# A buffer each for the two last rows, and fifteen tiny loads in the SyncE queue

## The chip, the cores and the metric

One core of a Trainium2 chip runs the whole kernel. The metric is device time in microseconds (us); several runs of one kernel are compared by their medians. A profile is one execution with the hardware profiler on; its span is the time between its first and last recorded instruction.

## The reference

A decode step of attention, forward and backward, with one query per head: 32 heads, 8192 keys and values of 128 numbers each, all bf16.

```python
B, H, Sq, Skv, Dh = 1, 32, 1, 8192, 128
scale = q.shape[-1] ** -0.5
scores = jnp.einsum('bhqd,bhkd->bhqk', q, k) * scale
attn = _softmax(scores, axis=-1)
out = jnp.einsum('bhqk,bhkd->bhqd', attn, v)
...
_out, _vjp = jax.vjp(_f, q, k, v)
return (_out, *_vjp(grad_out))     # O, dq, dk, dv
```

With p the softmax row, dp = v . dO and ds = p (dp - sum(p dp)) scale, the four results are O = p v, dq = ds k, dk = ds x q and dv = p x dO (two outer products). O and dq are 32 rows of 128 numbers, 8 KB each. K and V are read once (134 MB) and dk and dv written once (134 MB).

## The kernel before

The heads are taken in 16 pairs. A pair's K is one tile `Kt` of 128 partitions by 32 KB (4 MB), its V one tile `Vt` of the same shape; partitions 0 to 63 hold the first head, 64 to 127 the second. There are three K buffers and two V buffers. The outer products are written over the same tiles: `outer(j, "dk", r)` turns an eighth of `Kt` into dk and `outer(j, "dv", r)` an eighth of `Vt` into dv on VectorE, and behind the last eighth (or after each half, or quarter, in the first and last pairs) the finished tile is stored from SyncE (L271).

The loop `for j in range(HP + 1)` (L321) is written out by hand inside `tc.manual_schedule()`, so each engine executes in the order of the text. One turn j does the scores and the softmax of pair j, the gradient of K of pair j-1 (`p_`), and the V side of pair j. Nearly all transfers are issued from SyncE, in this order in a middle turn:

- the store of dk of pair j-1 (L271), which waits for VectorE's last `outer(p_, "dk", 7)`;
- `load_v(j + 1)` (L433, issued at L90), which waits until the store of dv of pair j-1 has landed, since it takes that buffer;
- the store of dv of pair j (L271), which waits for VectorE's last `outer(j, "dv", 7)`;
- `load_k(j + 2)` (L456, issued at L84), which waits until the store of dk of pair j-1 has landed.

SyncE's queue is in order: whatever waits there holds what stands behind it. The two loads of q and grad_out are the only transfers issued elsewhere (ScalarE, into `rows`). The built program gives its transfers eight completion counters in turn, so a transfer is issued only when the one eight issues before it (on the same counter) has landed.

Columns of O and dq gather in `o_all` and `dq_all` over the turns. The function `result(src, dst)` (L300 to L307) finishes one of them: ScalarE casts it into `half`, TensorE transposes it, ScalarE copies the 32 rows into `fin_sb` (L306), SyncE stores `fin_sb` (L307). Both `half` and `fin_sb` come from the pool `small`, which has one buffer for each name. `result(o_all, out_0)` is called in the last turn, j = 16 (L373), behind the eight `outer(p_, "dk", r)` of the last pair with their four stores of 1 MB; `result(dq_all, out_1)` follows at the end (L458).

Of the kernel before, what the change touches and what calls it, by code (L numbers as in the profile page):

```python
# [11 lines left out]
BF16 = mybir.dt.bfloat16  # L12
# [16 lines left out]
def kernel(  # L29
# [11 lines left out]
    nc = tc.nc  # L41
    P = 128
    _, H, S, D = k.shape
# [13 lines left out]
    consts = ctx.enter_context(tc.tile_pool(name="consts", bufs=1))  # L57
# [3 lines left out]
    small = ctx.enter_context(tc.tile_pool(name="small", bufs=1))  # L61
# [10 lines left out]
    def rows_of(x, j, c=0, parts=1):  # L72
        L = NT // parts
        return x[0, 2 * j:2 * j + 2].rearrange("b s d -> (b s) d").rearrange("(p n) d -> p n d", p=P)[:, c * L:(c + 1) * L, :]

    def slots(X, c, parts):
        L = NT // parts
        return X[:, c * L:(c + 1) * L, :]

    def load_k(j):  # L80
        Kt[j] = kpool.tile([P, NT, D], BF16, tag="K", name="Kt")
        parts = 4 if j == 0 else 1
        for c in range(parts):
            nc.sync.dma_start(slots(Kt[j], c, parts), rows_of(k, j, c, parts))  # L84

    def load_v(j):
        Vt[j] = vpool.tile([P, NT, D], BF16, tag="V", name="Vt")
        parts = 4 if j in (0, HP - 1) else 1
        for c in range(parts):
            nc.sync.dma_start(slots(Vt[j], c, parts), rows_of(v, j, c, parts))  # L90
# [6 lines left out]
    load_k(1)  # L97
    load_v(1)
    load_k(2)

    ident = consts.tile([P, P], BF16)
    make_identity(nc, ident[:])
# [99 lines left out]
    def v_scores(j, f):  # L202
        cols = XV[j].rearrange("p m s -> p (m s)").bitcast(BF16).rearrange(
            "p (m z s e) -> p z e m s", z=2, s=P, e=2)
        if f == 0:
            st[j]["dp"] = psD.tile([P, 512], F32, tag="dp", name="dp_ps")
        out = st[j]["dp"]
        for z in range(2):
            for e2 in range(2):
                at = 6 - 4 * f - 2 * z  # L210
                for b in range(NQ):
                    nc.tensor.matmul(out[b * QD:(b + 1) * QD, :], lhsT=do_win[:, b // 2, e2, at:at + QD],  # L212
                                     rhs=cols[:, z, e2, :, b * QD:(b + 1) * QD],
                                     start=(f == 0 and z == 0 and e2 == 0), stop=(f == 1 and z == 1 and e2 == 1),
                                     skip_group_check=True)
# [20 lines left out]
    def contract(j, which, first, last):  # L236
        X, pool = (Vt[j], psO) if which == "p" else (Kt[j], psQ)
        if first == 0:
            acc[which] = pool.tile([P, 512], F32, tag="acc", name="acc_" + which)
        for g in range(first, last):  # L240
            b = g % NQ
            nc.tensor.matmul(acc[which][b * QD:(b + 1) * QD, :], lhsT=wins[which][:, g, :],  # L242
                             rhs=X[:, 4 * g:4 * g + 4, :].rearrange("p n d -> p (n d)"),
                             start=(g < NQ), stop=(g >= NG - NQ), skip_group_check=True)
# [5 lines left out]
    def gather(j, which, bank):  # L250
        S, to = acc.pop("S" + which), (o_all if which == "p" else dq_all)
        pick = lane[:].rearrange("p (w j) -> p j w", j=4)
        at = 8 if which == "p" else 16
        for i in range(4):
            nc.tensor.matmul(bank[:, at:at + 2], lhsT=S[:, i, :], rhs=pick[:, i, 0:2],  # L255
                             start=(i == 0), stop=(i == 3), skip_group_check=True)
        nc.scalar.copy(to[:, 2 * j:2 * j + 2], bank[:, at:at + 2])

    def outer(j, which, r):
        x = st[j]  # L260
        G, dst = (Kt[j], out_2) if which == "dk" else (Vt[j], out_3)
        rep, row = x["ds"] if which == "dk" else x["p"], qd[j][:, 0 if which == "dk" else 1, :]
        nc.vector.tensor_tensor(  # L263
            slots(G, r, NU).rearrange("p n (a b) -> p n a b", b=R),
            slots(rep, r, NU).unsqueeze(2).to_broadcast([P, CH, D // R, R]),
            row.rearrange("p (a b) -> p a b", b=R).unsqueeze(1).to_broadcast([P, CH, D // R, R]),
            op=ALU.mult)
        parts = PARTS.get((which, j - HP), 2 if j < SPLIT else 1)
        if r % (NU // parts) == NU // parts - 1:
            c = r // (NU // parts)  # L270
            nc.sync.dma_start(rows_of(dst, j, c, parts), slots(G, c, parts))  # L271
# [26 lines left out]
        window("ds", ds1[:].rearrange("p (g j) -> p g j", j=4))  # L298

    def result(src, dst):  # L300
        half = small.tile([P, H], BF16, tag="half", name="half")
        nc.scalar.copy(half[:], src[:])
        fin_ps = psT.tile([P, 2 * TB, P], BF16, tag="T", name="fin_ps")
        nc.tensor.transpose(fin_ps[0:H, 0, :], half[:], ident[:])
        fin_sb = small.tile([H, D], BF16, tag="fin", name="fin_sb")
        nc.scalar.copy(fin_sb[:], fin_ps[0:H, 0, :])  # L306
        nc.sync.dma_start(dst.rearrange("b h s d -> (b h s) d"), fin_sb[:])  # L307

# [3 lines left out]
    def chunk(j, c):  # L312
        v_transposes(j, c)
        v_copy(j, c)
# [6 lines left out]
    for j in range(HP + 1):  # L321
# [50 lines left out]
        if j == HP:  # L372
            result(o_all, out_0)  # L373
            gather(p_, "ds", st[p_]["m"])
            break
# [53 lines left out]
        if not ends:  # L429
            for r in range(4, NU):  # L430
                outer(p_, "dk", r)
            if j + 1 < HP:
                load_v(j + 1)  # L433
        for r in range(NU):
            if early:
                contract(j, "p", 4 * r, 4 * r + 4)
                if 3 <= r < NU - 1:
                    for c in range(NC + 2 * r - 6, NC + 2 * r - 4):
                        if c > NC + 2:
                            chunk(j, c)  # L440
                if r == NU - 1:
                    v_scores(j, 1)
                    gather(p_, "ds", x["m"])
            else:
                for c in (2 * r, 2 * r + 1):
                    if j > 0 or c > 2:
                        chunk(j, c)
                contract(j, "p", 4 * r, 4 * r + 4)
                if r % 4 == 3:
                    v_scores(j, r // 4)  # L450
            outer(j, "dv", r)
# [2 lines left out]
            do_window(j + 1)  # L454
        if 0 < j and j + 2 < HP:
            load_k(j + 2)  # L456

    result(dq_all, out_1)  # L458
    order.__exit__(None, None, None)

# [29 lines left out]
```

## Time and profile before

| | |
|---|---|
| median of 3 runs | 640.74 us (640.11 to 641.88) |
| the profiled execution's own time | 640.61 us |
| its span | 638.5 us |
| busy, share of the span | PE 78%, DVE 81%, ACT 35%, POOL 1% |
| DMA packets of SyncE's and ScalarE's queues | 268.46 MB in 12480, 0.02 MB in 96 |
| read and written in HBM | 134.23 MB each, 420 GB/s over the span |

The profile's page gives the busy time of each engine, then the same in 40 slices of the span with the mean busy share of the core's 16 DMA engines, then the DMA queues, the chain of work that ended last, the costliest groups of instructions, and the transfers by the line that issues them with the median time from issue to landing. "SPq" is SyncE as an issuer of transfers, and the DMA queue q1 holds what SyncE issues, q10 what ScalarE issues; q8 and q14 bring instructions. Times in the views of waits, of stretches and of the timeline are microseconds from the start of the span.

### The profile page before, as it was taken

The page shows a single profiled execution, that of the slowest core. Times are in us where ns is not written, and L with a number is a line of the kernel's source. Part 1 is how long each engine was busy: PE and PEld are TensorE (multiplying, and loading weights), DVE is VectorE, ACT ScalarE, POOL GpSimd, SP SyncE. Part 2 cuts the span into 40 slices and gives each one's busy share as a digit, 9 for nine tenths or more (in the row PEclk, how much of TensorE's full clock was granted, in tenths as well). Part 3 has the DMA queues.
Part 4 walks back from the last instruction along what each step waited for, and adds up shares of the span by engine and source line. Part 5 has one row for each costly group of instructions (what it writes and reads, how often), then busy time and mean ns, then how long its engine had stood idle before and what let it go on. Part 6 is the DMA issues. An engine that isn't in the chain of part 4 may idle for free.

```text
span 638.5 us, 8533 instructions
## 1 busy us (share of the span) xinstructions
PE 498.9 (78%) x3480; PEld 282.3 (44%) x3480; DVE 517.1 (81%) x654; ACT 222.3 (35%) x508; POOL 3.2 (1%) x10
## 2 busy tenths in 40 slices
PE   4887786878787987879788778887779877788770
PEld 1444443354453635435264443635436354353540
DVE  6579997979889798877979877798777987968872
ACT  2432434053342614316053340524316243250440
POOL 2000000000000000000000000000000000000000
PEclk9789989878698886778968697796877968897685
DMA  8999999999999999999999999999999999999985
GB/s 365 436 437 405 440 424 431 415 424 435 437 429 431 428 428 431 432 441 430 426 427 429 443 432 429 426 430 439 434 432 426 429 438 427 436 431 422 404 371 220
DMA packets 12614, 269.01 MB, mean 421 GB/s; under 512 B 1568, under 2 KB 1568, under 8 KB 1568
## 3 DMA queue, kind: packets, MB, share of 16 engines
q1 hardware_dynamic: 12480, 268.46, 98.2%
q8 instruction: 27, 0.44, 0.3%
q14 instruction: 11, 0.09, 0.0%
q10 hardware_dynamic: 96, 0.02, 0.0%
HBM read 134.23 MB, written 134.23 MB: 420 GB/s over the span
## 4 chain that ended last, share of the span: by engine, by line
DMA 35%; PE 34%; DVE 23%; ACT 4%; issue 3%; DVEq 0%; SPq 0%; ACTq 0%
DMA Kt<-in_k_dram 19%; DMA out_dram<-Kt 15%; PE s_ps L178 13%; PE T_ps L195 9%; DVE Kt L263 8%; DVE XK_sb L168 6%; DVE Vt L263 4%; PE acc_ds L242 4%; PE m_ps L255 3%; PE acc_p L242 3%; DMA out_dram<-fin_sb 1%; DVE sT L185 1%; PE dp_ps L212 1%; ACT XV_sb L200 1%; DVE dpT L223 1%
## 5 line engine op out<-in xcount | busy, mean ns | idle before, releaser
L263 DVE TENSOR_TENSOR Vt<-p_rep,qd 128x2048 bf16<-128x2048 bf16 x128 | 155.6, 1224 | 58.2 <-PE acc_p L242 48.9
L178 PE MATMUL s_ps<-XK_sb,q_win 128*128 128x512 bf16 x512 | 151.5, 428 | 40.1 <-DVE XK_sb L168 34.8
L195 PE MATMUL T_ps<-ident_f,Vt 128*128 128x128 f32 x1024 | 169.5, 319 | 0.0
L200 ACT COPY XV_sb<-T_ps 128x512 f32<-128x512 f32 x256 | 140.2, 591 | 81.4 <-PE T_ps L195 81.3
L168 DVE STREAM_TRANSPOSE XK_sb<-Kt 128x1024 f32<-128x1024 f32 x128 | 151.0, 1221 | 21.0 <-DMA Kt<-in_k_dram 10.8
L263 DVE TENSOR_TENSOR Kt<-ds_rep,qd 128x2048 bf16<-128x2048 bf16 x128 | 149.5, 1215 | 3.2 <-PE acc_ds L242 2.8
L195 PEld LDWEIGHTS T_ps<-ident_f,Vt 128*128 128x128 f32 x1024 | 135.5, 164 | 36.6 <-issue 22.0
L178 PEld LDWEIGHTS <-q_win 128*128 128x128 bf16 x512 | 51.2, 110 | 124.2 <-issue 92.4
L242 PE MATMUL acc_p<-Vt,win_p 128*32 128x512 bf16 x512 | 56.0, 438 | 2.9 <-ACT win_p L234 2.9
L242 PE MATMUL acc_ds<-Kt,win_ds 128*32 128x512 bf16 x512 | 44.0, 441 | 4.6 <-ACT win_ds L234 4.6
L212 PE MATMUL dp_ps<-XV_sb,do_win 128*32 128x512 bf16 x512 | 34.6, 384 | 13.5 <-ACT XV_sb L200 13.5
L248 ACT COPY S_ds<-acc_ds 128x512 f32<-128x512 f32 x16 | 9.4, 587 | 84.1 <-PE acc_ds L242 84.1
L234 ACT COPY win_ds<-ds 64x128 bf16<-64x128 bf16 x32 | 9.5, 296 | 79.0 <-DVE ds L293 78.8
L404 ACT ACTIVATE e<-sT,nbias 128x128 f32<-128x128 f32 x16 | 8.3, 516 | 69.3 <-DVE nbias L400 69.3
L255 PE MATMUL m_ps<-lane,S_ds 128*128 128x2 f32 x128 | 25.1, 318 | 4.1 <-DVE rinv L414 4.1
L212 PEld LDWEIGHTS <-do_win 128*32 128x32 bf16 x512 | 14.2, 94 | 29.2 <-issue 22.6
L405 PE MATMUL m_ps<-rs,ones_f 128*128 128x1 f32 x32 | 8.0, 318 | 24.4 <-ACT e L404 24.4
L255 PEld LDWEIGHTS m_ps<-lane,S_ds 128*128 128x128 f32 x128 | 23.7, 277 | 6.2 <-DVE rinv L414 5.2
L242 PEld LDWEIGHTS <-win_p 128*32 128x32 bf16 x512 | 13.2, 94 | 28.3 <-issue 24.8
L242 PEld LDWEIGHTS <-win_ds 128*32 128x32 bf16 x512 | 9.8, 103 | 33.1 <-issue 30.0
L391 PE MATMUL m_ps<-ident_f,top 128*128 128x128 f32 x16 | 4.8, 300 | 23.6 <-DVE top L389 23.6
L185 DVE STREAM_TRANSPOSE sT<-s_ps 128x512 f32<-128x512 f32 x16 | 11.5, 717 | 14.2 <-PE s_ps L178 14.2
(59 smaller groups left out, 206.8 us busy)
## 6 DMA issues: line engine op xcount, KB each, us to landing
Kt<-in_k_dram SPq DMA_DIRECT2D x15, 4096.0 KB, 29.3
Vt<-in_v_dram SPq DMA_DIRECT2D x14, 4096.0 KB, 29.1
out_dram<-Vt SPq DMA_DIRECT2D x11, 4096.0 KB, 29.3
out_dram<-Kt SPq DMA_DIRECT2D x10, 4096.0 KB, 23.8
out_dram<-Vt SPq DMA_DIRECT2D x10, 2048.0 KB, 22.8
out_dram<-Kt SPq DMA_DIRECT2D x10, 2048.0 KB, 20.2
Vt<-in_v_dram SPq DMA_DIRECT2D x8, 1024.0 KB, 19.7
Kt<-in_k_dram SPq DMA_DIRECT2D x4, 1024.0 KB, 7.8
```

What stands on the lines that cost most here:

```text
L168: nc.vector.transpose(XK[j, u][:].rearrange("p g w i -> p (g w i)"), slots(Kt[j], u, NU).rearrange("p g d -> p (g d)").bitcast(F32))
L178: nc.tensor.matmul(st[j]["s"][:], lhsT=q_win[:, c, at:at + P], rhs=cols[:, c // 2, c % 2], start=(u == 0 and c == 0), stop=(u == NU - 1 an ...
L185: nc.vector.transpose(sT[:].rearrange("p g r -> p (g r)"), x["s"][:])
L195: nc.tensor.transpose(T_ps[:, i, :], words[:, m * P:(m + 1) * P], ident_f[:])
L200: nc.scalar.copy(XV[j][:, b * TB:(b + 1) * TB, :], st[j].pop(("T", c))[:])
L212: nc.tensor.matmul(out[b * QD:(b + 1) * QD, :], lhsT=do_win[:, b // 2, e2, at:at + QD], rhs=cols[:, z, e2, :, b * QD:(b + 1) * QD], start= ...
L234: nc.scalar.copy(wins[which][t * M:(t + 1) * M, :, 4 * t:4 * t + 4], src[t * M:(t + 1) * M])
L242: nc.tensor.matmul(acc[which][b * QD:(b + 1) * QD, :], lhsT=wins[which][:, g, :], rhs=X[:, 4 * g:4 * g + 4, :].rearrange("p n d -> p (n d) ...
L248: nc.scalar.copy(S[:].rearrange("p j d -> p (j d)"), acc.pop(which)[:])
L255: nc.tensor.matmul(bank[:, at:at + 2], lhsT=S[:, i, :], rhs=pick[:, i, 0:2], start=(i == 0), stop=(i == 3), skip_group_check=True)
L263: nc.vector.tensor_tensor(slots(G, r, NU).rearrange("p n (a b) -> p n a b", b=R), slots(rep, r, NU).unsqueeze(2).to_broadcast([P, CH, D // ...
L404: nc.scalar.activation(e[:].rearrange("p (u g) -> p u g", u=NU), x["sn"], ACT.Exp, bias=nbias[:], scale=scale, accum_out=rs[:])
```

## The change

Two things are changed.

- `half` and `fin_sb` in `result` get two buffers each, so the rows of dq no longer use the buffers of the rows of O.
- A new function `mark()` issues from SyncE a load of two numbers (4 bytes) into each of n partitions of a new tile `marked`, with n = 1 at the first call and 15 at the fifteenth. Nothing reads `marked`. From turn 6 on it is called right behind `load_v(j + 1)` and right behind `load_k(j + 2)`, until the fifteen are used up: two in each of the turns 6 to 12 and one in turn 13.

```diff
+    marks = list(range(1, 16))
+    marked = consts.tile([16, len(marks), 2], BF16)
+
+    def mark():
+        n = marks.pop(0)
+        nc.sync.dma_start(marked[0:n, n - 1], k[0, 0].rearrange("(p n) d -> p n d", p=P)[0:n, 0, 0:2])
...
     def result(src, dst):
-        half = small.tile([P, H], BF16, tag="half", name="half")
+        half = small.tile([P, H], BF16, tag="half", name="half", bufs=2)
         nc.scalar.copy(half[:], src[:])
         fin_ps = psT.tile([P, 2 * TB, P], BF16, tag="T", name="fin_ps")
         nc.tensor.transpose(fin_ps[0:H, 0, :], half[:], ident[:])
-        fin_sb = small.tile([H, D], BF16, tag="fin", name="fin_sb")
+        fin_sb = small.tile([H, D], BF16, tag="fin", name="fin_sb", bufs=2)
...
             if j + 1 < HP:
                 load_v(j + 1)
+                if j >= 6 and marks:
+                    mark()
...
         if 0 < j and j + 2 < HP:
             load_k(j + 2)
+            if j >= 6 and marks:
+                mark()
```

The order of instructions on TensorE, VectorE, ScalarE and GpSimd is the same in both programs; SyncE has fifteen transfers more. `marked` lies ahead of the big tiles in SBUF and moves all of them up by 64 bytes.

## The prediction

> **What bounds the kernel now.** I read the page first, then the DMA share by stretches of the span, then the tail: the chain, the timeline of ScalarE, the small tile that is stored last.
>
> ```profile
> span 638.5 us, 8533 instructions
> PE 498.9 (78%) x3480; PEld 282.3 (44%) x3480; DVE 517.1 (81%) x654; ACT 222.3 (35%) x508; POOL 3.2 (1%) x10
> ...
> DMA  8999999999999999999999999999999999999985
> ...
> q1 hardware_dynamic: 12480, 268.46, 98.2%
> q8 instruction: 27, 0.44, 0.3%
> ```
>
> No compute engine is over 81% busy; the packets of SyncE's queue fill 98.2% of 16 DMA engines over the whole span. In the 40 slices only the first and the last two are under 9. So transfers bound the kernel, and a change to it can bring something only where the DMA engines stand idle, which is at the two ends. The end, by stretches (the last two columns are the DMA share and GB/s):
>
> ```profile
> core 0: us, PE busy (x) PEld busy (x) DVE busy (x) ACT busy (x) POOL busy (x), PEclk, DMA share, GB/s
> ...
> 400.00:500.00 100.00, 82.83 (x582) 48.83 (x582) 82.12 (x102) 39.43 (x87) 0.00 (x0) 0.83 1.00 429
> ...
> 621.00:629.50 8.50, 1.50 (x10) 1.16 (x10) 5.21 (x5) 1.47 (x6) 0.00 (x0) 0.63 1.01 418
> 629.50:630.60 1.10, 0.00 (x0) 0.00 (x0) 0.00 (x0) 0.00 (x0) 0.00 (x0) 0.50 0.75 304
> 630.60:633.00 2.40, 0.00 (x0) 0.00 (x0) 0.00 (x0) 0.00 (x0) 0.00 (x0) 0.50 0.16 65
> 633.00:635.30 2.30, 0.00 (x0) 0.00 (x0) 0.00 (x0) 0.00 (x0) 0.00 (x0) 0.50 0.06 25
> 635.30:636.20 0.90, 0.00 (x0) 0.00 (x0) 0.00 (x0) 0.25 (x1) 0.00 (x0) 0.50 0.00 0
> ```
>
> In the middle all 16 engines work. From 629.5 on they run dry, and from 633.0 to 635.3 the share is 0.06, one engine of 16, at 25 GB/s, which is a sixteenth of some 430. So the DMA engines do not finish together: one is still working through its part of the last stores some 4.7 us after the first ones have run out (630.6 to 635.3). I call it the late ring. Nothing but its queue sets the time up to 635.8. What stands behind it:
>
> ```profile
> 626.66 9.15 DMA out_dram<-fin_sb
> 635.81 0.02 issue
> ...
> 635.89 0.25 ACT fin_sb L306
> ...
> L307 SPq DMA_DIRECT2D out_dram<-fin_sb x2: 319/450/581, 626.7 to 636.2; - x2
> ...
> DMA to landing us min/median/max: 1.3/5.2/9.1
> ...
> SPq L485 <- DMA out_dram<-fin_sb: 1.0, 1, 1.0
> ```
>
> The rows of O (8 KB) are issued at 626.66, behind the last 1 MB store in the same rings, and land 9.15 us later, when the late ring has come to them. Only then may ScalarE copy the rows of dq into the same `fin_sb` (635.89 to 636.14); their store is issued at 636.2, lands 1.3 us later, at 637.5, and the program ends 1.0 us after that, at 638.5.
>
> **The buffers: 1.65 us off the end.** The timeline of ScalarE shows how long dq had been ready:
>
> ```profile
> 622.18 0.25 ACT L306 COPY fin_sb<-fin_ps 32x128 bf16<-32x128 bf16 x1 [0.32 <-PE fin_ps L304]
> ...
> 623.36 0.22 ACT L302 CAST half<-dq_all 128x32 bf16<-128x32 f32 x1
> 635.89 0.25 ACT L306 COPY fin_sb<-fin_ps 32x128 bf16<-32x128 bf16 x1 [12.32 <-DMA out_dram<-fin_sb]
> ```
>
> The cast is done at 623.58. The copy of O started 0.32 us after its cast, so with a buffer of its own the copy of dq is over by 624.2, before SyncE issues the rows of O at 626.66. The rows of dq are then issued right behind them, by 627.6 at the latest (626.66 and two issues, 0.58 at most each, leave that much room), and stand in the rings directly behind the rows of O. What they add there is the price of a few small packets, which the stretch after 636.2 shows, since it holds nothing but the second of these stores:
>
> ```profile
> DMA packets 48, 0.01 MB, mean 4 GB/s; under 512 B 48, under 2 KB 48, under 8 KB 48
> ...
> q1 hardware_dynamic: 48, 0.01, 1.8%
> ...
> out_dram<-fin_sb SPq DMA_DIRECT2D x1, 8.0 KB, 1.3
> ```
>
> 48 packets took 1.8% of 16 x 2.3 us, 0.66 us, or 14 ns each; three to an engine (two rows and a completion count), so 0.04 us. The rows of dq land at 635.81 + 0.04 = 635.85, the end comes at 636.85, and 638.5 - 636.85 = 1.65 us go. From both sides: if they land together with the rows of O it is 1.7, and if a landing of its own 1.3 us were still to be paid behind the first it would be 638.5 - (635.81 + 1.3 + 1.0) = 0.4. I take 1.65, since four stores in a row are seen to pass through the rings without such gaps (share 1.01 from 621.0 to 629.5). What is late next is the late ring itself; the second buffers of `half` only remove a wait that already ends at 622.
>
> **The tiny loads in the rings: 0.2 us.** Fifteen loads have 1 + 2 + ... + 15 = 120 rows of 4 bytes. The trace of before has small loads at its start, those of q and grad_out, 32 rows of 256 bytes each; in the first 6 us:
>
> ```profile
> DMA packets 294, 1.54 MB, mean 257 GB/s; under 512 B 108, under 2 KB 108, under 8 KB 108
> ...
> q10 hardware_dynamic: 92, 0.02, 1.5%
> ```
>
> 1.5% of 96 us is 1.44 us for 92 packets, 16 ns each. A ring that takes part in a tiny load has one row and one count, 2 x 14 ns = 0.03 us. In the middle of the span that time is added to rings that are never idle, so it counts; and it decides the end only for the late ring. That ring has between 0 and all 15 of them: 0 to 0.42 us, and 0.2 at the half, which I take. These are lower bounds in one respect: a 4-byte load in the middle of full rings isn't in the trace of before. The upper bound is that a ring stands still until each load has landed, 1.3 us by the row above; it is a rival below. Less than nothing is excluded: nothing is taken off any ring.
>
> The Trainium skill ("DMA: Bandwidth & Descriptors", on why a DMA increments its semaphore by 16) says that a transfer from SyncE over n rows, n up to 15, runs on n engines, the lowest-numbered. By it the lowest engine takes part in all fifteen, and the charge would be 0.42 us if that is the late ring and 0 if the late one is the highest. No view here numbers the engines, so the trace neither bears it out nor speaks against it.
>
> **The tiny loads in SyncE's queue: nothing.** Each stands behind a big load and ahead of a store, and holds the store by its issue, 0.3 to 0.6 us by the row of L307 above. A middle turn in SyncE's timeline, and what it waits for between 240 and 560 us:
>
> ```profile
> 484.09 0.33 SPq L271 DMA_DIRECT2D out_dram<-Kt  x1
> 487.18 0.34 SPq L90 DMA_DIRECT2D Vt<-in_v_dram  x1
> 497.34 0.33 SPq L271 DMA_DIRECT2D out_dram<-Vt  x1
> 506.89 0.34 SPq L84 DMA_DIRECT2D Kt<-in_k_dram  x1
> 520.51 0.33 SPq L271 DMA_DIRECT2D out_dram<-Kt  x1
> ...
> SPq L271 <- DVE Kt L263: 131.3, 9, 16.8
> SPq L84 <- DMA out_dram<-Kt: 78.9, 8, 11.5
> SPq L271 <- DVE Vt L263: 71.0, 8, 11.0
> ```
>
> Behind the V load 10 us pass to the next store, behind the K load 13.6 us, and both stores wait for VectorE (131.3 us in 9 waits, 71.0 in 8). That cover is 20 times the issue. Were it gone, 15 x 0.33 = 5 us of issue would stand in the queue, though with two or three big transfers in the rings even those would not make them idle.
>
> The second thing in that queue is the completion counters. With six transfers to a turn instead of four, "eight issues before" goes back 1.33 turns instead of 2.
>
> ```profile
> Kt<-in_k_dram SPq DMA_DIRECT2D x15, 4096.0 KB, 29.3
> Vt<-in_v_dram SPq DMA_DIRECT2D x14, 4096.0 KB, 29.1
> out_dram<-Vt SPq DMA_DIRECT2D x11, 4096.0 KB, 29.3
> ```
>
> The closest case is the store of dk, which would look back to the K load of the turn before: the turn is 36.4 us long (484.09 to 520.51), that load was issued 36.4 + 13.6 = 50 us earlier and has landed after 29.3. 20 us of room, so no wait is added, and a later issue would need a landing of 50 us to be held.
>
> The third is the place of the tiles, 64 bytes higher in SBUF. I cost it at nothing: no row prices an address. If it lengthened or shortened each of the 12480 packets by one small packet's 14 ns, it would be 12480 x 14 ns / 16 = 11 us either way.
>
> **The sum.** Against the profiled execution: 640.61 - 1.65 + 0.2 = 639.16. It lies 0.13 under the median of the runs, so the forecast is 639.3 us, 0.22% less than 640.74. About 0.3%, or 1.9 us, is what a measurement of this kernel can tell from no change, and the forecast lies inside it.
>
> **Rivals.**
>
> *Each tiny load stops its rings until it has landed.* A mechanism that ends slower. For it: the only small store that stands alone in the trace takes 1.3 us from issue to landing with 0.04 us of packets. If the late ring takes part in all fifteen and loses 1.3 each time, 15 x 1.3 = 19.5 us are added: 640.74 + 19.5 - 1.65 = 658.6. It turns the sign at 1.65 / 15 = 0.11 us for each load, and makes the kernel slower by 0.3% from (1.65 + 1.9) / 15 = 0.24 us on. Against it: the share of 1.00 in the middle, where every big transfer, too, ends in a count of a few bytes in each ring without leaving the rings idle. Chance 0.13, mostly near the turning point, 642 to 645, and not at its upper end.
>
> [...]
>
> *The second buffer frees nothing.* The rows of dq land after the rows of O by a time of their own anyway, or the late ring is another, longer one in most runs, so that the end does not shorten: 0.4 us gained, 0.2 lost, 640.5. For it: SyncE's queue is in order and the two stores share rings. Against it: the stretch of 0.9 us at share 0.00 from 635.3 on, in which the rings wait for the second store and for nothing else. Chance 0.12.
>
> *Faster by over 0.3%.* The buffers bring their upper 1.7, the late ring has none of the tiny loads, and the end is as regular as in the profile: 639.0, which is 0.27% under the median. The runs of before spread over 1.8 us (640.11 to 641.88), so a measured difference of 0.3 to 0.4% is well within reach: 638.5. Chance 0.28.
>
> **The numbers.** The forecast proper, within 0.3%, has 0.47; with the rival that frees nothing, 0.59 for "same"; faster 0.28, slower 0.13. The range starts at the lowest run less the full gain, 640.11 - 1.7 = 638.4, and ends at the rival that frees nothing, 640.5, with half the spread of the runs, 0.9, on top: 641.4. It leaves out nearly all of the rival that stops the rings.
>
> **What would show it.** After: the chain still ends in the store of `fin_sb`, but ScalarE's second copy at L306 starts before 625 with no wait for a DMA; both stores of L307 stand within 1 us, and there is no stretch of share 0.00 before the last landing; from landing to the end 1.0 us remain. The DMA share in the middle stays 1.00, and the sixteen rings run dry at the same times as before, to 0.4 us. Wrong would be: idle stretches in the rings behind the tiny loads, a wait of SyncE at the tiny loads' line, a late ring that is later by over 0.5 us, or a last landing more than 0.5 us after the rows of O.

## The result and the profile after

638.6 us (six runs, 638.49 to 639.06) against 640.58 us for the kernel before in the same comparison: ratio 0.997, 95% interval 0.9957 to 0.9983. That is 2.0 us or 0.31% less, with an interval from 1.1 to 2.8 us. The forecast was 639.3 us, 0.22% less.

The page of the changed kernel: span, the DMA share in 40 slices, the packets by size, and the queues.

```profile
span 636.6 us, 8553 instructions
...
DMA  8999999999999999999999999999999999999995
...
DMA packets 12854, 269.01 MB, mean 423 GB/s; under 512 B 1808, under 2 KB 1808, under 8 KB 1808
...
q1 hardware_dynamic: 12720, 268.46, 98.6%
q8 instruction: 27, 0.44, 0.3%
```

The span is 1.9 us shorter. SyncE's queue has 240 packets more than before (12720 to 12480), the 120 rows and 120 counts of the tiny loads, and all slices but the first and the last are at 9. The last slice but one was an 8 before; that digit is not the change's, since the page of the same kernel run again (the full change once more, below) ends in an 8 and a 6. The same stretches of the middle and the tail as in the prediction:

```profile
400.00:500.00 100.00, 82.57 (x580) 48.77 (x581) 82.12 (x102) 39.41 (x87) 0.00 (x0) 0.83 1.01 432
...
621.00:629.50 8.50, 1.90 (x9) 1.62 (x9) 2.98 (x3) 0.73 (x4) 0.00 (x0) 0.50 0.91 381
629.50:630.60 1.10, 0.00 (x0) 0.00 (x0) 0.00 (x0) 0.00 (x0) 0.00 (x0) 0.50 0.33 142
630.60:633.00 2.40, 0.00 (x0) 0.00 (x0) 0.00 (x0) 0.00 (x0) 0.00 (x0) 0.50 0.14 56
633.00:635.30 2.30, 0.00 (x0) 0.00 (x0) 0.00 (x0) 0.00 (x0) 0.00 (x0) 0.50 0.04 18
```

In the middle, with the tiny loads in the rings, the share is 1.01; at the end one ring still works alone until about 635. The timelines of ScalarE and SyncE in the changed kernel (its lines L313, L314 and L278 are L306, L307 and L271 of the kernel before):

```profile
622.84 0.22 ACT L309 CAST half<-dq_all 128x32 bf16<-128x32 f32 x1
623.43 0.25 ACT L313 COPY fin_sb<-fin_ps 32x128 bf16<-32x128 bf16 x1 [0.38 <-PE fin_ps L311]
...
617.20 7.14 SPq L278 DMA_DIRECT2D out_dram<-Kt  x4
624.44 2.12 SPq L314 DMA_DIRECT2D out_dram<-fin_sb  x2
```

The copy of dq's rows stands at 623.43 with no wait for a DMA, where it stood at 635.89; both small stores are issued one behind the other, and after them there is no further step. By the counts of completion in the trace (sixteen for each big transfer and each row store, one from each ring), the rows of O land at 635.48 and the rows of dq at 635.67, against 635.81 and 637.52 before; 0.9 us later the program ends.

### The profile page after: what moved, and what is told of

It is laid out like the page before. It is cut to its first block, busy times and chain, and to the rows that moved or that the text cites. A ratio compares the mean times of both kernels' runs of the same rounds, so it can differ in the third digit from the quotient of the medians.

```text
span 636.6 us, 8553 instructions
## 1 busy us (share of the span) xinstructions
PE 498.7 (78%) x3480; PEld 283.3 (44%) x3480; DVE 518.0 (81%) x654; ACT 221.8 (35%) x508; POOL 3.2 (0%) x10
## 3 DMA queue, kind: packets, MB, share of 16 engines
q1 hardware_dynamic: 12720, 268.46, 98.6%
## 4 chain that ended last, share of the span: by engine, by line
PE 41%; DMA 26%; DVE 23%; ACT 4%; issue 3%; DVEq 0%; ACTq 0%; SPq 0%
DMA Kt<-in_k_dram 19%; PE s_ps L185 15%; PE T_ps L202 12%; DVE Kt L270 7%; DMA out_dram<-Kt 7%; DVE XK_sb L175 7%; PE acc_p L249 4%; PE acc_ds L249 4%; PE m_ps L262 3%; DVE Vt L270 3%; PE dp_ps L219 2%; ACT XV_sb L207 2%; DVE sT L192 1%; DVE dpT L230 1%; ACT p_rep L423 1%
## 5 line engine op out<-in xcount | busy, mean ns | idle before, releaser
L202 PE MATMUL T_ps<-ident_f,Vt 128*128 128x128 f32 x1024 | 167.2, 317 | 0.8 <-DMA Vt<-in_v_dram 0.8
L202 PEld LDWEIGHTS T_ps<-ident_f,Vt 128*128 128x128 f32 x1024 | 133.7, 163 | 36.9 <-issue 20.5
L249 PE MATMUL acc_ds<-Kt,win_ds 128*32 128x512 bf16 x512 | 42.5, 427 | 4.6 <-ACT win_ds L241 4.6
L219 PE MATMUL dp_ps<-XV_sb,do_win 128*32 128x512 bf16 x512 | 34.7, 386 | 13.5 <-ACT XV_sb L207 13.5
L262 PEld LDWEIGHTS m_ps<-lane,S_p 128*128 128x128 f32 x128 | 21.4, 240 | 5.7 <-issue 2.3
```

Source lines behind the costliest of these rows:

```text
L202: nc.tensor.transpose(T_ps[:, i, :], words[:, m * P:(m + 1) * P], ident_f[:])
```

## The experiments

All ratios are to the kernel before, run on the same chip beside the experiment.

### Each half of the change by itself

The buffers alone: `bufs=2` for `half` and `fin_sb`, no `mark()`.

> The second buffers of half and fin_sb alone, no tiny loads, no tile moved. Theory A (the buffers are the whole gain, the tiny loads cost and bring nothing): ratio 0.997, as the full change, about 638.6 us; in the profile the rows of dq land 0.2 us behind the rows of O and the program ends 0.9 to 1.0 us later. Theory B (the tiny loads, or the 64 bytes by which their tile moves the others, brought some 0.3 us of it): 638.9 to 639.2 us. Theory C (the tiny loads cost what was forecast, 0.2 us on the late ring): 638.4 us. B and C lie near what five rounds can resolve; a difference of over 0.6 us from the full change would be seen.

638.93 us, ratio 0.9981 (0.9972 to 0.9990): 1.2 us less than before, between 0.6 and 1.8. The tile that is stored last, in this kernel:

```profile
L306 ACT COPY fin_sb<-fin_ps x2: 254/254/254, 623.1 to 625.7; 32x128 bf16<-32x128 bf16 x2
L307 SPq DMA_DIRECT2D out_dram<-fin_sb x2: 608/862/1115, 626.7 to 627.4; - x2
...
DMA to landing us min/median/max: 8.2/8.4/8.7
```

The first store is issued at 626.7 and lands 8.7 us later, at 635.4; the second is issued at 627.4 and lands 8.2 us later, at 635.6. So the second costs 0.2 us behind the first.

The tiny loads alone: `mark()` and its calls, `half` and `fin_sb` with one buffer.

> The fifteen tiny loads alone, one buffer each for half and fin_sb as before. Theory A: the same as before, ratio 1.000 to 0.1%, and the profile ends as before with a stretch of share 0.00, ScalarE's wait of some 12 us and a second store. Theory B (they bring 0.3 us): 640.3 us. Rival, each tiny load stops its rings until it has landed: 642 us or more.

640.35 us, ratio 1.0003 (0.9994 to 1.0012). The fifteen loads cost between -0.4 and 0.8 us, at most 0.05 us each. ScalarE's wait for the first small store is back:

```profile
635.10 0.25 ACT L313 COPY fin_sb<-fin_ps 32x128 bf16<-32x128 bf16 x1 [9.97 <-DMA out_dram<-fin_sb]
```

Then a second buffer for `fin_sb` alone, and beside it the full change once more.

```diff
-        fin_sb = small.tile([H, D], BF16, tag="fin", name="fin_sb")
+        fin_sb = small.tile([H, D], BF16, tag="fin", name="fin_sb", bufs=2)
```

> A second buffer for fin_sb alone, one for half. Theory A (only the rows that a store still reads must be kept; the cast of dq waits for the transpose of O, done at 622): the same as both buffers, 638.9, ratio 0.998. Rival (the cast of dq is late too): the second store is issued later than 0.7 us behind the first.

> The full change once more, on the chip of these runs. Theory A (the buffers are all of it): ratio 0.998 as with the buffers alone, within 0.996 to 0.9990. Theory B (the tiny loads bring 0.1% of their own): 0.997 again, below 0.9975.

`fin_sb` alone: 638.67 us, ratio 0.9977 (0.9967 to 0.9986). The full change: 638.75 us, 0.9975 (0.9966 to 0.9984). The two cannot be told apart. The gain is that of one 256-byte-wide tile's second buffer; the second `half` and the tiny loads add nothing that these runs can see. Theory B, a gain from the tiny loads, isn't borne out: the ratio did not fall below 0.9975, and the loads alone gave 1.0003.

### Three times as many tiny loads

```diff
-        nc.sync.dma_start(marked[0:n, n - 1], k[0, 0]...[0:n, 0, 0:2])
+        for i in range(3):
+            nc.sync.dma_start(marked[0:n, 3 * (n - 1) + i], k[0, 0]...[0:n, 0, 0:2])
```

> The full change with each tiny load issued three times in a row (45 loads, ten transfers to a turn). Eight issues before then goes back less than a turn: the third tiny load behind the K load looks back to the V load of the same turn, which was issued some 20 us earlier and takes some 28 us to land, so SyncE must wait there for about 8 us; the third one behind the V load looks back to the K load of the turn before and waits for some 8 us too. Theory A (the queue has cover, since the store behind waits for VectorE 8 to 14 us after the load's issue): the waits stand in the trace, at the tiny loads' line, some 100 us in total, and the time is that of the full change to 0.3%, 638 to 640.5 us. Rival 1 (the counters bind): the stores behind are issued later than VectorE is done, and the time rises by some us. Rival 2 (rings stop for each tiny load): 30 more of them cost 30 times 0.1 us or more, 641.6 us and up.

639.49 us, ratio 0.9988 (0.9979 to 0.9997); the buffers alone gave 638.93 in the same comparison, so 45 tiny loads are worth 0.6 us, 0.012 us each, which the intervals do not tell from nothing. What SyncE waited for (L107 is the tiny load, L279 the store):

```profile
SPq L279 <- DVE Kt L271: 130.4, 21, 17.7
SPq L279 <- DVE Vt L271: 107.5, 15, 12.9
...
SPq L107 <- DMA Vt<-in_v_dram: 59.3, 7, 8.6
...
SPq L107 <- DMA Kt<-in_k_dram: 58.7, 7, 8.5
```

A turn of its timeline (L84 is the K load, L90 the V load):

```profile
508.57 0.35 SPq L84 DMA_DIRECT2D Kt<-in_k_dram  x1
508.97 9.57 SPq L107 DMA_DIRECT2D marked<-in_k_dram  x3
522.89 0.37 SPq L279 DMA_DIRECT2D out_dram<-Kt  x1
528.35 0.35 SPq L90 DMA_DIRECT2D Vt<-in_v_dram  x1
528.75 9.58 SPq L107 DMA_DIRECT2D marked<-in_k_dram  x3
538.44 0.37 SPq L279 DMA_DIRECT2D out_dram<-Vt  x1
```

The completion counters do bind here: 118 us of waits at the tiny loads' line, 8.5 us at a time. They take the place of waits for VectorE at the stores, of which 238 us remain. The profiled execution, at 640.9 us the slowest of its ten, shows where SyncE waited and not what that cost. Behind the K load 4.4 us of cover were left after the wait (518.5 to 522.9), behind the V load 0.1 us. This is where the counters would begin to cost, and the change as it stands is far from it: in its own trace SyncE has no wait at that line.

### The small stores ahead of the last big one

Buffers as above, no tiny loads, and the stores of `fin_sb` issued from ScalarE; run twice.

```diff
-        nc.sync.dma_start(dst.rearrange("b h s d -> (b h s) d"), fin_sb[:])
+        nc.scalar.dma_start(dst.rearrange("b h s d -> (b h s) d"), fin_sb[:])
```

> The second buffers, no tiny loads, and the two stores of fin_sb issued from ScalarE instead of SyncE. They are then issued as soon as their copies are done, at about 621 and 624 us, ahead of the last one or two stores of dk, and in another queue. Theory A (the end is the late ring, and the two small stores stand behind the last store of dk in it): the last landing becomes that of the last store of dk, 0.37 us earlier than with the buffers alone (635.67 to 635.30 in the profile of the full change); 638.2 us against 638.6. Rival (the second queue takes turns with the first in the same rings and costs elsewhere, or the end waits for something else): no gain, 638.6 or more.

> The second buffers and the small stores issued from ScalarE once more, beside the cut store, on the same chip: 638.0, ratio 0.9966 as before, 0.995 to 0.998.

637.99 us, ratio 0.9966 (0.9954 to 0.9979), and 638.07 us, 0.9963 (0.9951 to 0.9975). Each is the lowest of its comparison among the kernels that compute everything, 0.9 us under the buffers alone. The intervals of the two versions overlap, so the difference is likely and not shown; the two profiled executions lie 0.3 us apart (638.27 and 638.56). ScalarE's timeline:

```profile
620.65 0.33 ACTq L307 DMA_DIRECT2D out_dram<-fin_sb  x1
...
622.42 0.34 ACTq L307 DMA_DIRECT2D out_dram<-fin_sb  x1
```

They land 5.2 and 4.8 us later, at about 626 and 627, and the last landing is that of the last store of dk, at 635.45, 0.1 us ahead of the last one with the buffers alone (635.57). It did not cost nothing: SyncE waited 3.1 us for the counter of a small store before its last store of dk, which the late ring hid.

### Why one ring is late

Five runs with the instructions, the transfers and the computing changed. First fewer instructions on TensorE (the contractions take only the first 4 of 32 groups):

```diff
-        for g in range(first, last):
+        for g in range(first, min(last, NQ)):
```

> The second buffers, and of the 32 matmuls of each contraction (O and dq) only the first 4; the sums over the other 28 groups of rows are left out, so O and dq are not the reference's. TensorE has 3660 instructions instead of 5452, all bytes moved by the stores and loads are the same. Theory A (one ring is late because the instructions of TensorE are fetched through it, 16 KB at a time, 21 fetches in the whole kernel that put it some 10 us behind by 600 us, 0.5 us each): the q8 line shows 20 packets instead of 27, the late ring ends some 3.5 us earlier, and the time falls by 3 to 4 us against the buffers alone (638.9), to 635 to 636. Rival 1 (the late ring is slow by itself, or late from the partitions it serves): its end stays, 638.9 to 0.5 us, although TensorE has less to do. Rival 2 (compute sets the end): the stores of the last pair are issued earlier by the matmuls saved, about 2 x 28 x 0.14 = 8 us of TensorE time for a pair, less what is hidden, and the time falls by that whatever the ring does.

637.2 us, ratio 0.9953 (0.9938 to 0.9969), 1.5 us under the full change in the same comparison, not 3 to 4. SyncE's timeline:

```profile
614.65 7.14 SPq L271 DMA_DIRECT2D out_dram<-Kt  x4
```

The queue of instruction fetches on its page:

```profile
q8 instruction: 20, 0.33, 0.2%
```

And the last stretches:

```profile
630.60:633.00 2.40, 0.00 (x0) 0.00 (x0) 0.00 (x0) 0.00 (x0) 0.00 (x0) 0.50 0.10 42
633.00:635.30 2.30, 0.00 (x0) 0.00 (x0) 0.00 (x0) 0.00 (x0) 0.00 (x0) 0.50 0.01 4
```

The last four stores are issued from 614.65 on, 4.8 us earlier than before (619.42), and the time falls by a third of that. Compute does not set the end (rival 2 falls); the late ring does. The two runs with ScalarE's stores say the same without any change of the kernel, for SyncE issued the last four stores of dk 4.3 us apart in them:

```profile
617.83 8.40 SPq L271 DMA_DIRECT2D out_dram<-Kt  x4
622.14 8.31 SPq L271 DMA_DIRECT2D out_dram<-Kt  x4
```

The last landing came at 635.45 in the first and at 635.61 in the second. By the counts in the trace of the run with fewer matmuls, the late ring's part of the last store landed at 633.9 instead of 635.2 with the buffers alone: 1.3 us earlier, with 7 fetches less. That the fetches did it, and not the stores issued earlier, this run alone does not show.

More instructions: 200 memsets of a tiny tile on GpSimd in each of 13 turns.

```diff
+        if 0 < j < 14:
+            for i in range(200):
+                nc.gpsimd.memset(idle[:], 0.0)
```

> The second buffers, and 2600 tiny memsets on GpSimd spread over the turns 1 to 13 (GpSimd is idle there and nobody waits for them). Ten more fetches of 16 KB, so the q8 line shows about 37 packets. Theory A with GpSimd's fetches in another ring than TensorE's: a ring other than the late one falls back by 5 us, the late ring stays, and the time is 638.9 to 0.3%. Theory A with both in the same ring: the late ring falls back by 5 us more, 643.5 to 644. Rival (fetches cost the rings nothing): 638.9, and the rings run dry as with the buffers alone.

642.52 us, ratio 1.0037 (1.0023 to 1.0051), 3.6 us above the buffers alone. The fetches came in another queue than expected, q14, with 31 packets instead of 11, on the page:

```profile
q14 instruction: 31, 0.25, 0.1%
```

And the last stretches:

```profile
633.00:634.30 1.30, 0.00 (x0) 0.00 (x0) 0.00 (x0) 0.00 (x0) 0.00 (x0) 0.50 0.85 332
634.30:636.00 1.70, 0.00 (x0) 0.00 (x0) 0.00 (x0) 0.00 (x0) 0.00 (x0) 0.50 0.11 44
636.00:639.30 3.30, 0.00 (x0) 0.00 (x0) 0.00 (x0) 0.00 (x0) 0.00 (x0) 0.50 0.06 25
```

One ring now works alone until 639.3, 4 us longer than with the buffers alone. The other rings run dry later too, at 634.3 instead of 630.6, since the last four stores were issued later (619.45 with the buffers alone):

```profile
623.22 7.14 SPq L273 DMA_DIRECT2D out_dram<-Kt  x4
```

That this late issue is the cause is a rival; against it, an issue at 622.14 cost nothing above. And the counts of the V loads show when the ring fell behind. From the first of a load's sixteen counts to its last it is 4.0 us for the load issued at 65 us, 11.9 for the one at 374 and 13.5 for the one at 570; with the buffers alone 3.1, 6.3 and 9.2 for the same loads. The memsets end at about 401: the ring lost about 8 us instead of 3.2 while they ran, and 1.6 instead of 2.8 behind them. Twenty fetches of 8 KB more go with that; that the memsets themselves did it wasn't tried apart. The Trainium skill ("Runtime: NRT & Kernel Launch", on instruction fetch mechanics) calls the cost of going from one 16 KB block to the next mostly hidden. That speaks of the engine that runs the instructions, whose waits for a fetch no run here shows; what this run suggests is a cost on the other side, in a ring that is full.

Nothing computed: only the loads of K and V and the stores, in the same order.

> All loads of K and V and all stores of dk and dv in the same order and sizes, and nothing computed: the stores give back K and V, the two small outputs q and grad_out, so no output is the reference's. It asks why one ring is late. Theory A (the rings fall behind through the fetching of instructions): with some hundred instructions left there is nothing to fetch, the 16 rings run dry within 1 us of each other, and the time is that of the bytes, some 625 to 629 us. Rival (rings are late by themselves, from the partitions or the memory behind them): the DMA share still falls in steps over 4 us or more at the end, and the time is 630 to 636. Third (part of each, as the two runs with more and with fewer instructions suggest, since 7 fetches less moved the late ring by 1.3 us and 20 more by some 4): 2 to 4 us between the first and the last ring.

634.59 us, ratio 0.9899 (0.9881 to 0.9918). Its last stretches (this profile has no compute columns but GpSimd; the last two numbers are the DMA share and GB/s):

```profile
300.00:400.00 100.00, 0.00 (x0) 1.00 1.01 434
623.00:625.00 2.00, 0.00 (x0) 1.00 0.62 252
625.00:627.00 2.00, 0.00 (x0) 1.00 0.24 102
627.00:629.00 2.00, 0.00 (x0) 1.00 0.26 111
629.00:631.00 2.00, 0.00 (x0) 1.00 0.14 58
631.00:632.00 1.00, 0.00 (x0) 1.00 0.03 10
```

With one fetch of instructions in the whole run, four rings of 16 (share 0.25) still work when the others have run dry, and two of them (0.14) until 631. By the counts the last store of dk had landed in twelve rings by 625.0 and in the other four at 629.5, 629.9, 631.6 and 631.7. So the rival holds: the rings are late by themselves for the larger part, and what the two runs before put down to the fetches comes on top. What makes those four slower isn't settled by these runs.

Last, the late ring's queue was shortened. The version with ScalarE's stores, and the last 1 MB store of dk in four pieces:

```diff
+            to, frm = rows_of(dst, j, c, parts), slots(G, c, parts)
+            if which == "dk" and j == HP - 1 and c == parts - 1:
+                nc.sync.dma_start(to[:, 0:8, :], frm[:, 0:8, :])
+                for a, b in ((0, 64), (64, 121), (121, 128)):
+                    nc.sync.dma_start(to[a:b, 8:, :], frm[a:b, 8:, :])
```

> The version with the second buffers and the small stores issued from ScalarE, and the last quarter of the last store of dk cut up: a quarter of its columns over all 128 partitions as before, the other three quarters as 64, 57 and 7 partitions. In the full change's trace the late ring is the fifth from the lowest (the tiny load over 5 partitions is the first whose count comes late), and the first three rings run dry 4.6 us before it. 57 partitions divide by 3 and by no larger number up to 16; if such a store runs on the three lowest rings, the late ring has 5 packets of 6 KB instead of 8, 3 x 0.23 = 0.7 us less, and the three lowest rings 16 more, 3.7 us, for which they have room. Theory A (the late ring's queue is what sets the end): 0.7 us less than the same version without the cut, 637.3 against 638.0. Rival 1 (something else ends last): no change. Rival 2 (the 57 partitions go through rings that are not free, or one alone): 1 to 5 us more.

640.84 us, ratio 1.0007 (0.9991 to 1.0023): slower than the same version without the cut (638.07 in the same comparison). SyncE's waits after 610 us:

```profile
SPq L273 <- DMA out_dram<-fin_sb: 3.7, 1, 3.7
SPq L275 <- DMA out_dram<-fin_sb: 2.2, 1, 2.2
```

Its timeline, where L275 issues the pieces over 64, 57 and 7 partitions:

```profile
630.14 2.11 SPq L275 DMA_DIRECT2D out_dram<-Kt  x3
```

And a stretch of the end:

```profile
634.00:638.00 4.00, 0.00 (x0) 0.00 (x0) 0.00 (x0) 0.00 (x0) 0.00 (x0) 0.50 0.19 78
```

The share of 0.19 from 634 to 638 is three rings of 16, as the section cited in the prediction (the Trainium skill, "DMA: Bandwidth & Descriptors", on why a DMA increments its semaphore by 16) has it, by which a transfer runs on the largest number of engines up to 16 that divides its rows on both sides: 57 partitions divide by 3 and by no larger number up to 16. But two waits for the counters of the small stores put that store at 630.7, when its rings had run dry. Its 19 packets to a ring, 0.23 us each in the trace, are 4.4 us, and they ended at 638.2. The late ring's part, the store over 64 partitions, had landed by 633.95. With all small stores on SyncE again and the 57 partitions issued first:

> The second buffers with both small stores issued from SyncE, and the same cut of the last quarter of the last store of dk as before, but the 57 partitions issued first, so that no part of it waits for the count of a small store (the waits of SyncE at the cut were 3.7 and 2.2 us, and the 57 partitions were issued at 630.7, when the three lowest rings had already run dry). Theory A (the late ring sets the end, and the cut lost only by its late issue): the late ring ends 0.7 us earlier than with the buffers alone and the three lowest rings end with it, near 634.5; 638.2 us against 638.9, ratio 0.9965 to 0.998. Rival (stores over few rings run slower than 0.23 us for a packet of 6 KB, or hold what stands behind them): the three lowest rings end last again, 639.5 or more.

638.32 us, ratio 0.9975 (0.9966 to 0.9984); the forecast of 638.2 was for a late ring that ends 0.7 us earlier. In the trace its last part of dk landed at 634.5 to 634.7 instead of 635.2 to 635.5, and the rows of dq at 635.05. The size fits, the interval does not tell it from the buffers alone (0.9981).

## Why the prediction was right

**What bounds the kernel** was read rightly, and more firmly than the prediction could: in the profiled run of the changed kernel the last stores of dk happened to be issued 2.2 us earlier than before (617.20 to 619.42), and with most matmuls of the contractions left out 4.8 us earlier; the rows of O, behind the late ring, came 0.3 us earlier in the one and the time fell by 1.5 us in the other.

**The buffers, 1.65 us forecast.** The mechanism is the one forecast: no second round behind the late ring. The size: landing of dq minus landing of O went from 637.52 - 635.81 = 1.71 to 0.19 us, so 1.52 us. The step that was mis-sized is the price of the second store behind the first, 0.04 us by its packets; between the two landings it measured 0.19. The runs bracket 1.5: 1.2 us with the buffers alone, 1.5 for `fin_sb` alone (640.4 x 0.0023), 2.0 and 1.6 for the full change.

**The tiny loads, 0.2 us forecast** for the rings and nothing for SyncE's queue. Measured 0.2 us by the ratio 1.0003, with an interval from -0.4 to 0.8; that the two agree so well is luck. The rival in which each load stops its rings, 1.3 us for each load (0.24 would already have been a loss of 0.3%), falls by the same run: at most 0.05. The cover in SyncE's queue was there, and three times the loads show how much.

**The charge on the late ring** was put at half the loads for want of its number. The counts of the tiny loads in the trace number it: the load over 4 partitions is the last whose count comes before that of the late ring's big load, the load over 5 the first that comes with it, in this and two other kernels. If every load takes its rings in the same order, it took part in eleven of the fifteen, 0.3 us by the price of 0.03; too little to be seen in any run.

**The check of the rings** failed in the letter: the prediction had them run dry at the same times as before to 0.4 us. In the changed kernel's profile the share from 629.5 to 630.6 is 0.33 instead of 0.75, since that run had its last stores early; with the buffers alone it was 0.76, and 0.89 with the full change once more, whose last stores were issued from 619.56 on. It is run-to-run and not the change.

**The chance.** 0.31% less lies just outside "within 0.3%", the likeliest case of the forecast, and its interval (0.17 to 0.43%) covers both sides of that bound; three other runs of the same gain gave 0.19, 0.23 and 0.25%, inside it. The range held.

## What to carry over

Where transfers fill the span, don't stop at the share of 98%: ask when each DMA engine runs dry at the end, because the last one sets the time; 4.8 us of earlier stores brought 1.5, and 4.3 us of later ones cost nothing that could be seen. A small output that shares a buffer with another one waits until that one has landed behind the longest queue and pays a round of its own after it, here 1.2 to 2.0 us, so give it a buffer. Issuing it ahead of the last big store is likely worth some more, which these runs do not settle. Fifteen tiny transfers in full rings cost too little to be measured here, but each takes a completion counter, and a counter that comes round too early holds the queue behind it.

## What the runs showed of the hardware

The 16 DMA engines of a core did not keep step: with equal bytes, and nothing computed, the last store of dk landed in the first ring at 624.1 us and in the last one at 631.7 us into the span. The next small store behind another one in the same rings landed 0.2 us after it, against 1.3 us from issue to landing for one that is issued alone into empty rings. And 2600 more instructions on an idle engine went with 3.6 us, while one ring fell further behind the others as long as they ran; that their fetches did it is likely and not shown apart.
